# Other PSUM buffers, half steps, 128-wide stationary blocks and another order of work in an attention-plus-ELU-MLP kernel

## Chip, cores and metric

One core of one Trainium2 chip. The metric is the device time of one execution in microseconds (us). Profiled spans are some 2 us shorter than timed executions.

## The reference

Sliding-window attention with ALiBi over 8 batches of 8 heads, then a two-layer perceptron with ELU:

```python
scores = q @ k.T / sqrt(64)            # batch 8, heads 8, sequence 576, head dim 64
bias = slopes * -abs(rel)              # slopes 2**-(h+1)
mask = (rel >= 0) & (rel < 128)
attn = softmax(where(mask, scores + bias, -1e9))
x = (attn @ v)                         # to 4608 tokens x 512
h = x @ w_in                           # 512 -> 2048
g = where(h > 0, h, exp(min(h, 0)) - 1)
out = g @ w_out                        # 2048 -> 512, float32
```

The input is random; results are compared with this.

## The kernel before

Work goes out in slots. In each slot TensorE (PE) does a *hidden* step (16 matmuls of 128 columns or 8 of 256 into one 512-column PSUM bank), then attention tasks, then an *output* step. A hidden step is followed by an exponential on ScalarE (ACT), a clamp on GpSimd (POOL), and the ELU on VectorE (DVE), which reads the same PSUM bank once more. The ELU of step s-1 is issued after hidden step s.

```python
ps_s = tile_pool(name="ps_s", bufs=1, space=PSUM)     # sp: scores, 4 banks, one tile
ps_v = ...bufs=1   # av       ps_o = ...bufs=1   # op
ps_h = tile_pool(name="ps_h", bufs=2, space=PSUM)     # hp: a tile of one bank, twice
sp = ps_s.tile([128, 4, 512], F32, name="sp", tag="sp")
# ... cut ...
def hidden(t, c0, w, f0, nf):
    p = hps[t, c0, f0] = ps_h.tile([128, 512], F32, name="hp", tag="hp")
    # ... matmuls into p ...
    nc.scalar.activation(e[:, 0:n], p[:, 0:n], AF.Exp)
    nc.gpsimd.tensor_scalar(out=e[:, 0:n], in0=e[:, 0:n], scalar1=1.0, scalar2=0.0, op0=ALU.min, op1=ALU.max)

def elu(t, c0, w, f0, nf):
    V.scalar_tensor_tensor(out=gs[t][...], in0=sh(es.pop((t, c0, f0))), scalar=1.0,
                           in1=sh(hps.pop((t, c0, f0))), op0=ALU.subtract, op1=ALU.max)

def values(b, i, gp):                                 # block 4 of a batch has 64 rows
    m = 128 if i < 4 else 64
    parts = ([(unit(b, 3), 128, 3, 128), (unit(b, 3), 192, 4, 64)] if i == 4 else ...)
    # ... nc.tensor.matmul(a[0:m, g, h2, :], e[0:kk, 2*gp+g, h2, c:c+m], VP[...][0:kk, ...]) ...

for s in range(min(slots), max(slots) + 1):
    for f, a in early.get(s, []): f(*a)               # attention exponentials
    if s in HID: hidden(*HID[s])
    if s - 1 in HID: elu(*HID[s - 1])
    for f, a in tasks.get(s, []): f(*a)
    if s in OUT: output(*OUT[s])
```

The softmax here doesn't subtract the row's maximum and nothing guards it: scores larger than these inputs give would overflow.

## Time and profile before

| | before |
|---|---|
| median of 3 executions | 360.79 us (360.69 to 361.33) |
| profiled span | 358.8 us |
| PE busy | 332.8 us, 93% |
| to the first hidden step | 18.12 us |
| first hidden step to first output step (slots 0 to 17) | 34.08 |
| slots 18 to 33 | 18.34 |
| slots 34 to 47 (batch 1's block) | 34.30 |
| slot 48 to the start of the last hidden step (slot 159) | 237.78 |
| rest | 16.18 |

The stages are read from the order of time on PE: the start of the first hidden matmul, the first output matmul, and so on.

### The profile page before, as it was taken

How to read it: one execution, taken by the hardware profiler on the slowest of the kernel's cores; microseconds unless marked ns; L12 is line 12 of the kernel's file. 1: busy time of each engine (PE TensorE's matmuls, PEld its weight loads, DVE VectorE, ACT ScalarE, POOL GpSimd, SP SyncE). 2: the span in 40 equal slices, each digit the busy share in tenths (PEclk: the TensorE clock that was granted, in tenths of full speed). 3: DMA queues.
4: the chain of work that ended last, by engine and by line, in shares of the span. 5: the costliest groups of instructions: out<-in, count | busy, mean ns of one | idle time of the engine just before them, and what ended most of it. 6: DMA issues, size and time to landing. Idle time of an engine off the chain costs nothing.

```text
span 358.8 us, 8891 instructions
## 1 busy us (share of the span) xinstructions
PE 332.8 (93%) x3706; PEld 230.7 (64%) x3706; DVE 223.3 (62%) x443; ACT 175.4 (49%) x313; POOL 172.8 (48%) x261
## 2 busy tenths in 40 slices
PE   8898879856999999999999999999999999999994
PEld 8687664445676666766667666666677666666641
DVE  5445536479668866786669756786679566654320
ACT  1645344554455545554666255555556365533421
POOL 9336459254466536562666456562656133332320
PEclk9879999999999999999999999999999999999999
DMA  9998349995577838994899649991999311111011
GB/s 111 195 188 110 36 41 134 190 151 38 65 107 94 91 64 104 107 97 69 93 112 94 78 67 123 100 98 39 136 115 102 61 45 46 46 45 38 29 60 58
DMA packets 97320, 32.10 MB, mean 89 GB/s; under 512 B 87040, under 2 KB 92672, under 8 KB 97280
## 3 DMA queue, kind: packets, MB, share of 16 engines
q0 software_dynamic: 76480, 18.36, 60.2%
q1 hardware_dynamic: 20800, 13.18, 13.1%
q8 instruction: 29, 0.48, 0.5%
q14 instruction: 11, 0.09, 0.1%
HBM read 36.70 MB, written 9.44 MB: 129 GB/s over the span
## 4 chain that ended last, share of the span: by engine, by line
PE 68%; DVE 10%; ACT 8%; DMA 4%; issue 4%; POOL 4%; ACTq 0%; DVEq 0%; POOLq 0%
PE hp L225 26%; PE op L247 25%; PE av L189 9%; DVE g L238 5%; ACT EX L173 5%; PE sp L167 4%; POOL e L231 3%; ACT e L230 3%; DMA wo<-in_moe_w_out_dram 2%; DMA out_dram<-ob 2%; PE spare L257 2%; DVE EX L179 2%; DVE KT L127 1%; PE sp L148 1%; DVE QT L127 1%
## 5 line engine op out<-in xcount | busy, mean ns | idle before, releaser
L231 POOL TENSOR_SCALAR e<-e 128x512 f32<-128x512 f32 x144 | 93.5, 650 | 167.1 <-ACT e L230 166.3
L225 PE MATMUL hp<-xT,wi 128*128 128x256 f16 (+3 forms) x1600 | 151.0, 243 | 12.8 <-DVE g L238 9.4
L225 PEld LDWEIGHTS <-wi 128*128 128x128 f16 x1600 | 122.3, 98 | 52.4 <-issue 17.3
L247 PE MATMUL op<-wo,g 128*128 128x512 f16 x576 | 145.3, 379 | 2.6 <-ACT ob L251 1.4
L230 ACT ACTIVATE e<-hp 128x512 f32<-128x512 f32 x144 | 87.2, 605 | 115.0 <-PE hp L225 112.6
L238 DVE SCALAR_TENSOR_TENSOR g<-e,hp 128x512 f16<-128x512 f32 x144 | 96.9, 673 | 55.9 <-POOL e L231 54.4
L247 PEld LDWEIGHTS <-g 128*128 128x128 f16 x576 | 50.7, 97 | 48.2 <-issue 7.8
L173 ACT ACTIVATE EX<-sp 128x512 f16<-128x512 f32 (+1 forms) x121 | 69.8, 634 | 15.9 <-PE sp L167 10.1
L179 DVE TENSOR_TENSOR EX<-EX,TAB 128x1024 f16<-128x1024 f16 x56 | 39.1, 699 | 29.5 <-ACT EX L173 29.5
L189 PE MATMUL av<-VP,EX 128*128 128x65 f16 (+1 forms) x576 | 44.4, 200 | 2.5 <-ACT EX L173 1.3
L189 PEld LDWEIGHTS <-EX 128*128 128x128 f16 (+1 forms) x576 | 34.7, 100 | 12.6 <-issue 3.1
L251 ACT COPY ob<-op 128x512 f32<-128x512 f32 x36 | 21.1, 586 | 40.6 <-PE op L247 38.4
L198 DVE TENSOR_TENSOR xn<-av,rden 128x256 f16<-128x256 f32 (+1 forms) x80 | 33.8, 423 | 2.7
L93 POOL DMA_DIRECT2D VP<-in_v_dram x40 | 35.0, 879 | 0.7 <-issue 0.6
L197 DVE RECIPROCAL rden<-av 128x4 f32<-128x4 f32 (+1 forms) x80 | 14.1, 176 | 24.1 <-PE av L189 23.9
L127 DVE STREAM_TRANSPOSE KT<-st 128x576 f16<-128x576 f16 x28 | 22.5, 814 | 0.0
L127 DVE STREAM_TRANSPOSE QT<-st 128x576 f16<-128x576 f16 x28 | 22.3, 807 | 0.0
L167 PE MATMUL sp<-QT,KT 32*128 32x256 f16 (+2 forms) x560 | 18.3, 250 | 2.7 <-ACT EX L173 2.7
L87 POOL DMA_DIRECT2D st<-in_q_dram x28 | 19.1, 681 | 2.7 <-DMA wo<-in_moe_w_out_dram 2.1
L87 POOL DMA_DIRECT2D st<-in_k_dram x28 | 19.2, 689 | 0.7 <-DMA VP<-in_v_dram 0.6
L167 PEld LDWEIGHTS <-KT 32*128 32x128 f16 (+1 forms) x560 | 10.5, 95 | 5.9 <-issue 4.2
L257 PE MATMUL spare<-ident 128*128 128x128 f16 x90 | 6.6, 249 | 1.6 <-DVE ident L282 1.6
(33 smaller groups left out, 60.8 us busy)
## 6 DMA issues: line engine op xcount, KB each, us to landing
out_dram<-ob SPq DMA_DIRECT2D x36, 256.0 KB, 2.4
VP<-in_v_dram POOLq DMA_DIRECT2D x32, 128.0 KB, 4.0
st<-in_k_dram POOLq DMA_DIRECT2D x28, 144.0 KB, 3.6
st<-in_q_dram POOLq DMA_DIRECT2D x28, 144.0 KB, 3.5
wi<-in_moe_w_in_dram POOLq DMA_DIRECT2D x4, 512.0 KB, 11.1
wo<-in_moe_w_out_dram POOLq DMA_DIRECT2D x4, 512.0 KB, 6.1
VP<-in_v_dram POOLq DMA_DIRECT2D x8, 64.0 KB, 3.2
xT<-xn SPq DMA_TRANSPOSE x32, 3.4
```

Source lines behind the costliest of these rows:

```text
L87: nc.gpsimd.dma_start(st[b][32 * g:32 * g + 32, w, :, :, :, :].rearrange("p h n j d -> p (h n) (j d)"), (q, k)[w][b, 2 * g:2 * g + 2, :, : ...
L93: nc.gpsimd.dma_start(VP[b % 2][0:p, n, :, 0:D], v[b, :, 128 * n:128 * n + p, :].rearrange("h p d -> p h d"))
L127: V.transpose(o, st[b][:, w, h2, :, :, 32 * dh:32 * dh + 32])
L167: nc.tensor.matmul(sp[0:m, g, 256 * h2 + o:256 * h2 + o + n], kt[r, h2, dh, 128 * kb:128 * kb + m], qt[r, h2, dh, q0:q0 + n], start=dh == ...
L173: nc.scalar.activation(unit(b, u)[:, g0:g1, :, c0:c1], sp[:, g0:g1, :].rearrange("p g (h c) -> p g h c", h=2)[:, :, :, c0:c1], AF.Exp, sca ...
L179: V.tensor_tensor(out=e, in0=e, in1=TAB[:, int(u == 3), 2 * gp:2 * gp + 2, :, :], op=ALU.mult)
L189: nc.tensor.matmul(a[0:m, g, h2, :], e[0:kk, 2 * gp + g, h2, c:c + m], VP[b % 2][0:kk, n, 4 * gp + 2 * g + h2, 0:D + 1], start=j == 0, sto ...
L225: nc.tensor.matmul(p[:, l * w + u0:l * w + u1], w_in_sb[:, c, fc * 128:(fc + 1) * 128], xT[:, c, x0:x0 + u1 - u0], start=(c == 0), stop=(c ...
L230: nc.scalar.activation(e[:, 0:n], p[:, 0:n], AF.Exp)
L231: nc.gpsimd.tensor_scalar(out=e[:, 0:n], in0=e[:, 0:n], scalar1=1.0, scalar2=0.0, op0=ALU.min, op1=ALU.max)
L238: V.scalar_tensor_tensor(out=gs[t][:, f0:f0 + nf, c0:c0 + w], in0=sh(es.pop((t, c0, f0))), scalar=1.0, in1=sh(hps.pop((t, c0, f0))), op0=A ...
L247: nc.tensor.matmul(o, gs[t][:, fc, ts * 128:(ts + 1) * 128], w_out_sb[:, fc, :], start=(fc == 0), stop=(fc == NFC - 1))
```

## The change

The intent: hidden steps of batch 0 get four PSUM buffers instead of two (two banks of sp are lent to them, and scores of batch 0 then use the other two, four heads at a time); in batch 1's block each step is cut in two halves, each with half a bank; all stationary blocks are made 128 columns wide, with zeroed padding, so that matmuls of the last block need not change form; the second transposes of batch 0 move behind the first hidden step, and several loads are issued earlier.

```diff
-    ps_h = ctx.enter_context(tc.tile_pool(name="ps_h", bufs=2, space=PSUM))
+    ps_h = ctx.enter_context(tc.tile_pool(name="ps_h", bufs=1, space=PSUM))
...
     sp = ps_s.tile([128, 4, 512], F32, name="sp", tag="sp")
+    hp = ps_h.tile([128, 2, 512], F32, name="hp", tag="hp")
...
-            parts = ([(unit(b, 3), 128, 3, 128), (unit(b, 3), 192, 4, 64)] if i == 4 else
+            parts = [(3, 128, 3), (3, 192, 4)] if i == 4 else [(i, 0, i)] + ...
-                            a[0:m, g, h2, :], e[0:kk, 2 * gp + g, h2, c:c + m],
-                            VP[b % 2][0:kk, n, 4 * gp + 2 * g + h2, 0:D + 1],
+                        nc.tensor.matmul(a[:, x, h2, :], ex_[u][:, c:c + 128], VP[b % 2][:, n, 2 * g + h2, 0:D + 1],
...
-        def hidden(t, c0, w, f0, nf):
-            p = hps[t, c0, f0] = ps_h.tile([128, 512], F32, name="hp", tag="hp")
+        def hidden(t, c0, w, f0, nf, p):
+            hps[t, c0, f0] = p
-            e = es[t, c0, f0] = work.tile([128, 512], F32, name="e", tag="e")
+            e = es[t, c0, f0] = work.tile([128, 512], F32, name="e", tag="e", bufs=6)
...
+        BUF = [hp[:, 0, :], hp[:, 1, :], sp[:, 2, :], sp[:, 3, :]]
+        HALF = [hp[:, i, 256 * j:256 * j + 256] for i in range(2) for j in range(2)]
         for s, (sub, f) in enumerate(first):
-            HID[s] = (0, 128 * sub, 128, 4 * f, 4)
+            HID[s] = [(0, 128 * sub, 128, 4 * f, 4, BUF[s % 2 if s < 4 else s % 4])]
...
-            HID[34 + f] = (1, 64, 128, 4 * f, 4)
+            HID[34 + f] = [(1, 64, 128, 4 * f + 2 * i, 2, HALF[2 * (f % 2) + i]) for i in range(2)]
...
-                HID[16 * t + 16 + j] = (t, 256 * (j // 8), 256, 2 * (j % 8), 2)
+                HID[16 * t + 16 + j] = [(t, 256 * (j // 8), 256, 2 * (j % 8), 2, BUF[j % 2])]
```

Left out: scores and exponentials of batch 0 by half, the padding memsets, the new slots of tasks and loads, output buffers given as banks.

More of the change, by code (lines that the diff above doesn't have):

```diff
@@ L61 @@
     QT = [one([128, 2, 2, S], F16, f"QT{i}") for i in range(2)]
-    KT = [one([128, 2, 2, S], F16, f"KT{i}") for i in range(2)]
+    kt_ = [one([128, 4 * S + 64], F16, f"KT{i}") for i in range(2)]
+    KT = [t[:, 0:4 * S].rearrange("p (a b s) -> p a b s", a=2, b=2) for t in kt_]
     Q0, K0 = [t[0].rearrange("p a b s -> p (a b) s") for t in (QT, KT)]
     VP = [one([128, 5, H, VW], F16, f"VP{i}") for i in range(2)]
-    EX = [one([128, 4, 2, 256], F16, f"EX{i}") for i in range(4)]
+    ex_ = [one([128, 2048 + 64], F16, f"EX{i}") for i in range(4)]
+    EX = [t[:, 0:2048].rearrange("p (g h c) -> p g h c", g=4, h=2) for t in ex_]
     w_in_sb = one([128, 4, FF], F16, "wi")
@@ L103, in load_wo, with turn_first @@
             moe_w_out[512 * i:512 * i + 512, :].rearrange("(c p) d -> p c d", p=128))
-    def turn_first(w, part, half, tag):
-        pool = {"hp": ps_h, "av": ps_v, "op": ps_o}[tag]
+    def turn_first(w, part, half, bank):
         n, nh = ((64, 2), (32, 4))[part]
-        t = pool.tile([128, nh, 6, n], F16, name="tp", tag=tag)
+        if bank is None:
+            bank = ps_o.tile([128, DO], F32, name="tp", tag="op")
+        t = bank.bitcast(F16)[:, 0:nh * 6 * n].rearrange("p (x j r) -> p x j r", x=nh, j=6)
         r = slice(64 * part, 64 * part + n)
@@ L138, in unit @@
             return EX[u]
-        def scores(b, u):
-            qt, kt = QT[b % 2], KT[b % 2]
-            parts = ([(0, u, 128 * u, 256)] if u < 3 else [(0, 3, 384, 192), (192, 4, 512, 64)])
-            if b == 0:
-                for part, (o, kb, q0, n) in enumerate(parts):
-                    m = 128 if kb < 4 else 64
-                    for h2 in range(2):
-                        for g in range(4):
-                            nc.tensor.matmul(
-                                sp[0:m, g, 256 * h2 + o:256 * h2 + o + n], SI[:, 2 * g + h2, 0:m], RB[:, 0:n],
-                                start=part == h2 == 0, stop=False, skip_group_check=True)
-                for o, kb, q0, n in parts:
-                    m = 128 if kb < 4 else 64
-                    for x in range(4):
-                        for hh in range(2):
-                            r, h = slice(64 * hh, 64 * hh + 64), 4 * hh + x
-                            c = 256 * (h % 2) + o
-                            nc.tensor.matmul(
-                                sp[0:m, h // 2, c:c + n], K0[r, x, 128 * kb:128 * kb + m], Q0[r, x, q0:q0 + n],
-                                start=False, stop=True, skip_group_check=True)
-                return
-            for o, kb, q0, n in parts:
-                m = 128 if kb < 4 else 64
@@ new lines, in blocks, with first_scores @@
+        def blocks(u):
+            return [(0, u, 128 * u, 256)] if u < 3 else [(0, 3, 384, 192), (192, 4, 512, 64)]
+        def first_scores(u, half, d):
+            heads = [(x, hh) for x in (2 * half, 2 * half + 1) for hh in range(2)]
+            for part, (o, kb, q0, n) in enumerate(blocks(u)):
+                for x, hh in heads:
+                    c = 256 * (x % 2) + o
+                    nc.tensor.matmul(sp[:, 2 * d + hh, c:c + n], SI[:, 4 * hh + x, :], RB[:, 0:n],
+                                     start=part == x % 2 == 0, stop=False, skip_group_check=True)
+            for o, kb, q0, n in blocks(u):
+                for x, hh in heads:
+                    r, c = slice(64 * hh, 64 * hh + 64), 256 * (x % 2) + o
+                    k0 = x * S + 128 * kb
+                    nc.tensor.matmul(sp[:, 2 * d + hh, c:c + n], kt_[0][r, k0:k0 + 128], Q0[r, x, q0:q0 + n],
+                                     start=False, stop=True, skip_group_check=True)
@@ L163, in scores, with first_expo @@
+        def first_expo(u, half, d, c0, c1):
+            nc.scalar.activation(
+                unit(0, u)[:, half::2, :, c0:c1],
+                sp[:, 2 * d:2 * d + 2, :].rearrange("p g (h c) -> p g h c", h=2)[:, :, :, c0:c1], AF.Exp, scale=0.125)
+        def scores(b, u):
+            for o, kb, q0, n in blocks(u):
                 for h2 in range(2):
@@ L166, in scores, with expo @@
                             r = slice(32 * g, 32 * g + 32)
+                            k0 = (2 * h2 + dh) * S + 128 * kb
                             nc.tensor.matmul(
-                                sp[0:m, g, 256 * h2 + o:256 * h2 + o + n], kt[r, h2, dh, 128 * kb:128 * kb + m],
-                                qt[r, h2, dh, q0:q0 + n], start=dh == 0, stop=dh == 1,
+                                sp[:, g, 256 * h2 + o:256 * h2 + o + n], kt_[b % 2][r, k0:k0 + 128],
+                                QT[b % 2][r, h2, dh, q0:q0 + n], start=dh == 0, stop=dh == 1,
                                 tile_position=(32 * g, 0))
-        def expo(b, u, g0, g1, c0=0, c1=256):
-            nc.scalar.activation(
-                unit(b, u)[:, g0:g1, :, c0:c1],
-                sp[:, g0:g1, :].rearrange("p g (h c) -> p g h c", h=2)[:, :, :, c0:c1], AF.Exp, scale=0.125)
+        def expo(b, u, g):
+            nc.scalar.activation(unit(b, u)[:, g, :, :], sp[:, g, :].rearrange("p (h c) -> p h c", h=2),
+                                 AF.Exp, scale=0.125)
         def weigh(b, u, gp):
@@ L179, in weigh, with values @@
             V.tensor_tensor(out=e, in0=e, in1=TAB[:, int(u == 3), 2 * gp:2 * gp + 2, :, :], op=ALU.mult)
-        def values(b, i, gp):
+        def values(b, i, part):
             m = 128 if i < 4 else 64
-            parts = ([(unit(b, 3), 128, 3, 128), (unit(b, 3), 192, 4, 64)] if i == 4 else
-                     [(unit(b, i), 0, i, 128)] + ([(unit(b, i - 1), 128, i - 1, 128)] if i else []))
+            banks = (part, part + 2) if b == 0 else (2 * part, 2 * part + 1)
+            parts = [(3, 128, 3), (3, 192, 4)] if i == 4 else [(i, 0, i)] + ([(i - 1, 128, i - 1)] if i else [])
@@ L185, in values @@
             a = ps_v.tile([128, 2, 2, D + 1], F32, name="av", tag="av")
-            for g in range(2):
+            for x, g in enumerate(banks):
                 for h2 in range(2):
-                    for j, (e, c, n, kk) in enumerate(parts):
-                        nc.tensor.matmul(
-                            a[0:m, g, h2, :], e[0:kk, 2 * gp + g, h2, c:c + m],
-                            VP[b % 2][0:kk, n, 4 * gp + 2 * g + h2, 0:D + 1],
-                            start=j == 0, stop=j == len(parts) - 1)
@@ L193, in values @@
-            if gp == 0:
-                xnt[b, i] = work.tile([128, 2, 4, D], F16, name="xn", tag="xn", bufs=6)
-            r = work.tile([128, 4], F32, name="rden", tag="rden", bufs=2)
-            af = a.rearrange("p g h d -> p (g h) d")
-            V.reciprocal(out=r[0:m, :], in_=af[0:m, :, D])
-            V.tensor_tensor(out=xnt[b, i][0:m, gp, :, :], in0=af[0:m, :, 0:D],
-                            in1=r[0:m, :].unsqueeze(2).broadcast_to([m, 4, D]), op=ALU.mult)
+                    for j, (u, c, n) in enumerate(parts):
+                        c += 512 * g + 256 * h2
+                        nc.tensor.matmul(a[:, x, h2, :], ex_[u][:, c:c + 128], VP[b % 2][:, n, 2 * g + h2, 0:D + 1],
+                                         start=j == 0, stop=j == len(parts) - 1)
@@ new lines, in values @@
+            if part == 0:
+                xnt[b, i] = work.tile([128, 4, 2, D], F16, name="xn", tag="xn", bufs=6)
+            o = xnt[b, i][0:m, part::2, :, :] if b == 0 else xnt[b, i][0:m, 2 * part:2 * part + 2, :, :]
+            r = work.tile([128, 2, 2], F32, name="rden", tag="rden", bufs=2)
+            V.reciprocal(out=r[0:m], in_=a[0:m, :, :, D])
+            V.tensor_tensor(out=o, in0=a[0:m, :, :, 0:D], in1=r[0:m].unsqueeze(3).broadcast_to([m, 2, 2, D]),
+                            op=ALU.mult)
@@ L203, in turn @@
             o = (b * S + 128 * i) % RING
-            x = xnt.pop((b, i)).rearrange("p a h d -> p (a h d)")
+            x = xnt.pop((b, i)).rearrange("p g h d -> p (g h d)")
             if dma:
@@ L232, in hidden, with elu @@
                                     op0=ALU.min, op1=ALU.max)
-        def elu(t, c0, w, f0, nf):
+        def elu(t, c0, w, f0, nf, p):
             if t not in gs:
@@ L240, in elu, with output @@
                 in1=sh(hps.pop((t, c0, f0))), op0=ALU.subtract, op1=ALU.max)
-        def output(t, ts, f0, pool=None, tag="op"):
+        def output(t, ts, f0, bank=None, av=False):
             if f0 == 0:
-                ops[t, ts] = (pool or ps_o).tile([128, DO], F32, name="op", tag=tag)
+                ops[t, ts] = (bank if bank is not None else ps_v.tile([128, DO], F32, name="oa", tag="av") if av else
+                              ps_o.tile([128, DO], F32, name="op", tag="op"))
             o = ops[t, ts]
@@ L274 @@
         load_wi(1)
-        for n in (2, 3, 4):
-            load_v(0, n)
+        load_v(0, 2)
         load_wi(2)
+        load_v(0, 3)
+        load_v(0, 4)
         load_wi(3)
+        load_wo(0)
+        load_wo(1)
         rowf = one([128, 1], F32, "rowf")
@@ L284 @@
             V.memset(VP[i][:, :, :, D:D + 1], 1.0)
+            V.memset(VP[i][64:128, 4, :, 0:D], 0.0)
+            V.memset(kt_[i][:, 4 * S:4 * S + 64], 0.0)
+        for e in ex_:
+            V.memset(e[:, 2048:2112], 0.0)
         ra = one([128, 512], F32, "ra")
@@ L299 @@
         warm(90)
-        turn_first(1, 0, 0, "hp")
-        turn_first(0, 0, 0, "hp")
-        turn_first(1, 0, 1, "op")
-        turn_first(0, 0, 1, "av")
-        scores(0, 0)
-        expo(0, 0, 0, 2, 0, 128)
-        expo(0, 0, 2, 4, 0, 128)
-        expo(0, 0, 0, 4, 128, 256)
+        turn_first(1, 0, 0, hp[:, 0, :])
+        turn_first(0, 0, 0, hp[:, 1, :])
+        turn_first(1, 0, 1, None)
+        turn_first(0, 0, 1, sp[:, 3, :])
+        for half in range(2):
+            first_scores(0, half, half)
+        for half in range(2):
+            first_expo(0, half, half, 0, 128)
+        for half in range(2):
+            first_expo(0, half, half, 128, 256)
         values(0, 0, 0)
-        turn_first(1, 1, 0, "hp")
-        turn_first(0, 1, 0, "hp")
         values(0, 0, 1)
-        scores(0, 1)
-        expo(0, 1, 0, 4, 0, 128)
-        expo(0, 1, 0, 4, 128, 256)
         turn(0, 0, False)
-        values(0, 1, 0)
+        for half in range(2):
+            first_scores(1, half, half)
+        for half in range(2):
+            first_expo(1, half, half, 0, 128)
         early, tasks, HID, OUT = {}, {}, {}, {}
@@ L325, in before @@
             early.setdefault(s, []).append((f, a))
-        first = [(0, 0), (0, 1), (1, 0), (1, 1), (2, 0), (2, 1), (0, 2), (1, 2),
-                 (2, 2), (3, 0), (3, 1), (3, 2), (0, 3), (1, 3), (2, 3), (3, 3)]
+        BUF = [hp[:, 0, :], hp[:, 1, :], sp[:, 2, :], sp[:, 3, :]]
+        HALF = [hp[:, i, 256 * j:256 * j + 256] for i in range(2) for j in range(2)]
+        first = [(0, 0), (0, 1), (1, 0), (1, 1), (0, 2), (1, 2), (2, 0), (2, 1),
+                 (2, 2), (0, 3), (1, 3), (2, 3), (3, 0), (3, 1), (3, 2), (3, 3)]
         for s, (sub, f) in enumerate(first):
-            HID[s] = (0, 128 * sub, 128, 4 * f, 4)
+            HID[s] = [(0, 128 * sub, 128, 4 * f, 4, BUF[s % 2 if s < 4 else s % 4])]
         for f in range(2):
-            HID[16 + f] = (1, 0, 64, 8 * f, 8)
+            HID[16 + f] = [(1, 0, 64, 8 * f, 8, BUF[2 + f])]
         for f in range(4):
             for ts in range(4):
-                pool, tag = ((ps_o, "op"), (ps_v, "av"), (ps_h, "hp"), (ps_h, "hp"))[ts]
-                OUT[18 + 4 * f + (ts if f < 3 else (1, 0, 2, 3)[ts])] = (0, ts, 4 * f, pool, tag)
+                OUT[18 + 4 * f + (ts if f < 3 else (1, 0, 2, 3)[ts])] = (
+                    0, ts, 4 * f, BUF[ts - 2] if ts > 1 else None, ts == 1)
         for f in range(4):
-            HID[34 + f] = (1, 64, 128, 4 * f, 4)
-            HID[40 + f] = (1, 256, 128, 4 * f, 4)
-            HID[44 + f] = (1, 384, 128, 4 * f, 4)
+            HID[34 + f] = [(1, 64, 128, 4 * f + 2 * i, 2, HALF[2 * (f % 2) + i]) for i in range(2)]
+            HID[40 + f] = [(1, 256, 128, 4 * f + 2 * i, 2, HALF[2 * (f % 2) + i]) for i in range(2)]
+            HID[44 + f] = [(1, 384, 128, 4 * f, 4, BUF[f % 2])]
         for f in range(2):
-            HID[38 + f] = (1, 192, 64, 8 * f, 8)
+            HID[38 + f] = [(1, 192, 64, 8 * f + 4 * i, 4, HALF[2 * f + i]) for i in range(2)]
         for t in range(2, NTB):
             for j in range(16):
-                HID[16 * t + 16 + j] = (t, 256 * (j // 8), 256, 2 * (j % 8), 2)
+                HID[16 * t + 16 + j] = [(t, 256 * (j // 8), 256, 2 * (j % 8), 2, BUF[j % 2])]
         for t in range(1, NTB):
@@ L348 @@
                 OUT[16 * t + 26 + j] = (t, j // 4, 4 * (j % 4))
+        at(0, turn_first, 1, 1, 0, hp[:, 1, :])
+        at(0, values, 0, 1, 0)
+        at(0, turn_first, 0, 1, 0, None)
         at(0, values, 0, 1, 1)
-        at(0, scores, 0, 2)
-        before(1, expo, 0, 2, 0, 4, 0, 128)
+        for half in range(2):
+            before(1, first_expo, 1, half, half, 128, 256)
         at(1, turn, 0, 1, False)
-        before(2, expo, 0, 2, 0, 4, 128, 256)
-        at(2, values, 0, 2, 0)
-        at(3, values, 0, 2, 1)
@@ L358 @@
-        at(3, scores, 0, 3)
-        before(4, expo, 0, 3, 0, 4, 0, 128)
-        before(4, turn, 0, 2, False)
-        before(5, expo, 0, 3, 0, 4, 128, 256)
-        at(5, values, 0, 3, 0)
-        at(6, values, 0, 3, 1)
-        at(7, values, 0, 4, 0)
-        at(7, turn, 0, 3, False)
-        at(8, values, 0, 4, 1)
-        at(9, turn, 0, 4, False)
+        at(1, first_scores, 2, 0, 0)
+        at(1, first_scores, 2, 1, 1)
+        before(2, first_expo, 2, 0, 0, 0, 128)
+        before(2, first_expo, 2, 1, 1, 0, 128)
@@ new lines @@
+        before(3, first_expo, 2, 0, 0, 128, 256)
+        before(3, first_expo, 2, 1, 1, 128, 256)
+        at(3, values, 0, 2, 0)
+        at(3, values, 0, 2, 1)
+        at(3, first_scores, 3, 0, 0)
+        at(4, turn, 0, 2, False)
+        before(5, first_expo, 3, 0, 0, 0, 128)
+        before(6, first_expo, 3, 0, 0, 128, 256)
+        at(6, first_scores, 3, 1, 0)
+        at(7, values, 0, 3, 0)
+        before(7, first_expo, 3, 1, 0, 0, 128)
+        before(8, first_expo, 3, 1, 0, 128, 256)
@@ L368 @@
+        at(8, values, 0, 3, 1)
+        at(9, values, 0, 4, 0)
+        at(9, turn, 0, 3, False)
+        at(10, values, 0, 4, 1)
+        at(11, turn, 0, 4, False)
         for h in range(H):
             at(17 + h, table, h)
-        at(0, load_wo, 0)
-        at(2, load_wo, 1)
-        for n, s in enumerate((3, 4, 5, 6)):
+        for n, s in enumerate((2, 3, 5, 5)):
             at(s, load_qk, 1, 1, n)
-        for n, s in enumerate((8, 11, 14, 16)):
+        for n, s in enumerate((6, 8, 11, 14)):
@@ L377 @@
             at(s, load_qk, 1, 0, n)
-        at(17, load_wo, 2)
-        at(18, load_v, 1, 0)
-        at(19, load_v, 1, 1)
-        at(20, load_wo, 3)
-        for n in range(3):
-            at(21 + n, load_v, 1, 2 + n)
+        at(15, load_wo, 2)
+        at(16, load_wo, 3)
+        for n in range(5):
+            at(17 + n, load_v, 1, n)
         for n in range(4):
-            at(19 + n, turn_qk, 1, 1, *divmod(n, 2))
-            at(23 + n, turn_qk, 1, 0, *divmod(n, 2))
+            at(18 + n, turn_qk, 1, 1, *divmod(n, 2))
+            at(22 + n, turn_qk, 1, 0, *divmod(n, 2))
@@ L391 @@
             for g in range(4):
-                before(a + 1 + (2 * g) // 3, expo, 1, u, g, g + 1)
+                before(a + 1 + (2 * g) // 3, expo, 1, u, g)
             at(a + 2, weigh, 1, u, 0)
@@ L409 @@
                 for g in range(4):
-                    before(a + 1 + g // 2, expo, b, u, g, g + 1)
+                    before(a + 1 + g // 2, expo, b, u, g)
                 at(a + 1, weigh, b, u, 0)
@@ L432 @@
                 f(*a)
-            if s in HID:
-                hidden(*HID[s])
-            if s - 1 in HID:
-                elu(*HID[s - 1])
+            for step in HID.get(s, []):
+                hidden(*step)
+            for step in HID.get(s - 1, []):
+                elu(*step)
             for f, a in tasks.get(s, []):
```

## The prediction

> **What bounds the kernel now.** I read the page first, then busy time by stage, then the waits inside the stages, then the order of time on TensorE (PE). The kernel works in slots: one step of the first layer (hidden, L225), the ELU of the step before, attention tasks, one step of the second layer (output, L247).
>
> Page, parts 1 and 2:
>
> ```profile
> PE 332.8 (93%) x3706; PEld 230.7 (64%) x3706; DVE 223.3 (62%) x443; ACT 175.4 (49%) x313; POOL 172.8 (48%) x261
> PE   8898879856999999999999999999999999999994
> PEclk9879999999999999999999999999999999999999
> ```
>
> PE is the bound from the 11th slice on; only the first quarter has holes. No other engine is over 62%. Busy time by stage (columns: stretch, length, then busy us of PE, weight load, DVE, ACT, POOL, granted clock, DMA share, GB/s), cut at the first hidden step, the first output, batch 1's block (slot 34), slot 42, slot 48 and the last hidden step:
>
> ```profile
> 0.00:18.12 18.12, 15.23 (x334) 13.02 (x335) 8.76 (x24) 7.15 (x9) 11.33 (x22) 0.91 1.25 153
> 18.12:52.20 34.08, 27.95 (x444) 24.25 (x442) 17.08 (x37) 14.32 (x22) 16.60 (x27) 0.95 0.75 96
> 52.20:70.54 18.34, 16.32 (x114) 7.44 (x111) 9.95 (x18) 9.51 (x19) 11.96 (x17) 1.00 1.45 145
> 70.54:92.70 22.16, 14.94 (x304) 12.69 (x303) 18.11 (x36) 12.35 (x24) 10.06 (x15) 1.00 0.78 97
> 92.70:104.84 12.14, 12.03 (x137) 8.29 (x137) 7.58 (x17) 5.87 (x12) 5.88 (x10) 1.00 0.73 100
> 104.84:343.50 238.66, 236.36 (x2341) 160.77 (x2341) 160.69 (x313) 123.85 (x227) 116.37 (x171) 1.00 0.68 81
> ```
>
> From 92.7 to 343.5 PE is busy 99%: there the time is what PE issues, nothing else. In 70.5 to 92.7 DVE (18.1 of 22.2) is nearer the bound than PE. In 18 to 52 neither is full: waits rule. The timeline of PE in the long stage shows what its work costs:
>
> ```profile
> 122.76 0.41 PE L189 MATMUL av<-VP,EX 128*128 128x65 f16 x8
> 123.01 1.02 PE L247 MATMUL op<-wo,g 128*128 128x512 f16 x4
> 126.50 1.04 PE L225 MATMUL hp<-xT,wi 128*128 128x256 f16 x8
> 127.47 1.24 PE L189 MATMUL av<-VP,EX 128*64 128x65 f16 x8
> 128.64 1.04 PE L247 MATMUL op<-wo,g 128*128 128x512 f16 x4
> ```
>
> Start to start, eight ordinary value matmuls take 123.01 - 122.76 = 0.25 us, 31 ns each. The eight for the last, 64-row block of a batch start 0.10 late (127.47 after a hidden step that issues in 0.87) and take 1.17. A closer look shows why: the two forms alternate, with 0.14 to 0.15 us from one to the next:
>
> ```profile
> 127.62 0.36 PE L189 MATMUL av<-VP,EX 64*64 64x65 f16 x2
> 127.76 0.36 PE L189 MATMUL av<-VP,EX 128*64 128x65 f16 x2
> ```
>
> Narrowness alone is not it: in batch 0's scores eight 64-column blocks of one form run together and load in 0.33 us, 41 ns each:
>
> ```profile
> 27.53 0.33 PEld L148 LDWEIGHTS <-SI 128*64 128x64 f16 x8 [0.16 <-issue]
> ```
>
> The waits of 18 to 52 us and of 70.5 to 92.7 us (total, times, longest) show the hidden buffers coming back late, and in the second stretch one chain: an output transfer, held up, blocks an ACT copy, behind it an exponential, behind it PE:
>
> ```profile
> PE hp L225 <- DVE g L238: 4.8, 8, 1.0
> ...
> PE sp L167 <- ACT EX L173: 2.5, 1, 2.5
> ACT ob L251 <- DMA out_dram<-ob: 2.2, 1, 2.2
> ```
>
> In slots 10 to 17 the hidden steps start at 41.80, 43.16, 44.96, 46.32, 48.11 us: 1.58 a slot, for 0.9 of work. A step plus ACT 0.60, POOL 0.61 and DVE 0.69 with hand-overs is 3.1 us, over two buffers 1.58.
>
> **What the Trainium skill says.** (1) "TensorEngine Tiling (Array Packing)", Tiling Modes, Key Properties: changing the tiling mode, not just the tile, drains TensorE. The trace agrees: 146 ns where row or column size changes at every matmul, 31 where it doesn't. (2) "TensorE: Matmul & The Clock Gate", Weight-path perf modes: the fast weight load needs 128 columns, so padding could help by that as well; the 41 ns above say that this part is small here. (3) The same page, Part 1, The HAM clock gate: a PE with little to do for some 3.4 us falls to half clock. The trace agrees: granted clock 0.50 in 15 to 21 us. (4) "PSUM — Partial Sum Buffer", PSUM bank collisions raise a hardware error: two engines may not be in one bank and quadrant at once. This matters for the half steps, which put two halves in one bank; no run yet shows what it costs.
>
> **The change part by part.**
>
> *All blocks 128 wide.* Every value matmul becomes 128*128. A last-block call falls from 0.10 + 1.17 = 1.27 to 0.25, saved 1.02; where scores follow, from 1.26 to 0.34, saved 0.92. In the long stage there are 2 calls in each of 6 batches: 12 x 0.98 = 11.8. The scores of unit 3 take 0.69 against 0.55 for other units; I give back 0.07 in each of 6: 0.4. PE is on the path there, so it all counts. DVE: at 126.27 it had caught up, waiting for POOL, and idled 1.79 before the slow call's result, so it can follow; average load goes from 67% to 71%. For its local queues I take off 0.4. **Long stage: -11.8.** Batch 1's two calls (91.56, 94.59) count below, batch 0's two are PE time as well (-1.8, below). The filling memsets (about 1.3 us of DVE by my estimate) lie in DVE's 1.76 us wait for the iota.
>
> *Batch 0: four heads at a time, second transposes after the first step, four buffers.* The first hidden step starts at 18.12, behind two groups of 96 transposes, scores of units 0 and 1, and three exponentials. New path: transposes end at 9.9; scores half by half to 11.3; exponentials to 12.4; values, DVE 0.6, turn 0.6, copy 0.42: 14.2; meanwhile scores of unit 1 (2 us, at half clock 3) hold PE to 16.2. So 1.9 earlier. From there to slot 18 PE has: 18 hidden x 0.9 = 16.2; 8 value calls 3.1; moved transposes 1.9; scores of units 2 and 3 4.0; turns 1.6: 26.8. With four buffers in slots 4 to 17 the 3.1 us chain allows 0.78 a slot, under PE's 0.9; POOL, with 0.61 a slot and five DMA issues of 0.7 to 0.8 in ten slots, needs 0.98. I add 2.0 for the half clock, which the gap of PE between 11.3 and 13.5 will bring again, and 0.4 for waits: 29.2. Slot 18 at 16.2 + 29.2 = 45.4, against 52.2. **First part: -6.8.**
>
> *Issues in other slots.* The second-layer weights were waited for twice (0.41 and 0.67 before outputs): the second half goes out at slots 15 and 16, before V, and both waits go. Ahead of slot 34 I leave the ACT and PSUM hand-over around slot 31 (0.9 us), which the order keeps. **Output stretch: -1.2**, 0.1 for the shorter queue. The wait for the output transfer (2.2) should fall to 0.5 or so, as batch 2's loads, issued at 59 to 68 us in its way, go out well before relative to a less crowded queue.
>
> *Half steps in slots 34 to 43.* Two 256-column instructions for each of 512. My estimates from rows of the profile: DVE 0.42 each (a 256-column PSUM read takes 425 ns) against 0.673, so +0.17 a slot; ACT 0.40 each (610 ns at 512 and 1022 at 1024), +0.2; POOL 0.40, +0.2. Ten slots: +1.7 on DVE, the fullest engine here. If one bank is kept to one engine, the second half's matmuls wait for the first half's exponential: 0.45 + 0.2 + 0.40 + 0.45 = 1.5 us in PE in place of 0.9, and where an attention exponential stands ahead on ACT, more. So: stall -1.7, DVE +1.7, ordering +0.8, the two last-block calls -1.5 (one of them beside a DVE queue). **Batch 1 block: -0.7.**
>
> Sum: -6.8 - 1.2 - 0.7 - 11.8 = -20.5, and 360.8 - 20.5 = **340.3 us**.
>
> **The rivals.** *A: DVE takes over.* If DVE is what sets slots with transposes, some of the 11.8 comes back as waits of hidden for the ELU. For: slots 51 to 57 show DVE without a gap and waits of 0.2. Against: it has caught up one slot before the slow calls. It would make 343 to 346. *B: the half steps stall PE bank by bank*, and each slot takes 2.7 instead of 2.2: +4, 344 to 345. For: the bank rule and the full DVE; against: PE has slack there. *C: the start runs at full clock and the half steps pipeline freely*: 2 from the clock, 2 from the block, and the transfer stall gone: 334 to 336. *D: narrow blocks cost by width and the drain stays*, because scores in 32-row tiles still alternate with 128-row work: then the 11.8 hardly shows and 352 results. Against it stand the 41 ns.
>
> **Range and chances.** The long stage is measured on PE itself, +-1. The first part is a chain of my own sums, +-3; the block +-3. Together some +-5, with rivals A and B above and C below: 334 to 347. Faster by 2% means under 353.6: even with no gain before 104 us the last-block calls alone give 349, so 0.96; within 2% 0.03; slower 0.01.
>
> **What would show it.** Right: value matmuls all 128*128 and 0.25 us per eight; the stretch from slot 48 to the last hidden step 11 to 12.5 shorter than 238.7; hidden steps of slots 10 to 17 at 0.9 to 1.0 apart; first hidden near 16, first output near 45, no wait for the second-layer weights. Wrong: hidden waiting for the ELU more than 1.2 us in the long stage (A); PE idle between the halves of a step, slots 34 to 43 over 24 us (B); or last-block values still near 1.2 us (D).

## The result

| | before | after |
|---|---|---|
| median | 360.74 us (4 executions) | 442.14 us (440.69 to 445.3, 4 executions) |
| to the first hidden step | 18.12 | 21.91 |
| slots 0 to 17 | 34.08 | 45.16 |
| slots 18 to 33 | 18.34 | 18.81 |
| slots 34 to 47 | 34.30 | 47.67 |
| slot 48 to last hidden step | 237.78 | 290.22 |
| rest | 16.18 | 16.13 |

The ratio is 1.226 (95% interval 1.220 to 1.233). The change is slower by 81 us, where 20 us faster was forecast, and the prediction gave slower a chance of 0.01. Two thirds of the loss (52.4) lie in the long stage, the stage that the prediction held to be the safest.

The page after, parts 1 and 2:

```profile
PE 343.2 (78%) x3706; PEld 232.1 (53%) x3706; DVE 226.3 (51%) x461; ACT 179.1 (41%) x330; POOL 169.5 (39%) x271
PE   7785669766788888778888877778888877787775
PEclk9678999965599999999999999999999999999999
```

No engine got more work to speak of: DVE 226 us for 223, ACT 179 for 175, PE the same 3706 matmuls (343 us for 333; the difference arose where the granted clock was lower, see below). PE is down to 78% busy, evenly over the whole long stage, so it waits in every slot. The busy time of two stages (columns as in the prediction: stretch, length, busy us of PE, weight load, DVE, ACT, POOL, clock, DMA share, GB/s):

```profile
85.88:118.43 32.55, 22.49 (x305) 19.08 (x305) 17.29 (x40) 12.06 (x29) 11.79 (x23) 0.59 0.38 37
133.55:424.80 291.25, 235.93 (x2341) 154.58 (x2341) 162.49 (x312) 125.27 (x227) 110.23 (x170) 1.00 0.48 66
```

In the long stage PE does the same 236 us of work as before in 291. What it waits for is in the waits of the whole run (us in total, times, longest; PEld is the weight load, and "issue" means that it waited for nothing that the profile shows). First the changed kernel, then the kernel before:

```profile
DVE g L246 <- ACT e L238: 171.5, 137, 4.4
PEld L233 <- issue: 101.6, 115, 1.7
PE hp L233 <- DVE g L246: 64.7, 99, 1.5
```

```profile
DVE g L238 <- POOL e L231: 54.4, 76, 1.9
PE hp L225 <- DVE g L238: 9.4, 20, 1.0
```

Before, the ELU on DVE waited for POOL's clamp, which makes its input, and PE waited 9.4 us in all for the ELU. Now the ELU waits for an *exponential on ACT*. The timeline of one slot shows which one:

```profile
391.13 1.03 PE L233 MATMUL hp<-xT,wi 128*128 128x256 f16 x8 [0.37 <-DVE g L246]
392.20 0.60 ACT L238 ACTIVATE e<-hp 128x512 f32<-128x512 f32 x1 [0.78 <-PE hp L233]
392.88 0.61 POOL L239 TENSOR_SCALAR e<-e 128x512 f32<-128x512 f32 x1 [1.90 <-ACT e L238]
392.89 0.69 DVE L246 SCALAR_TENSOR_TENSOR g<-e,hp 128x512 f16<-128x512 f32 x1 [1.27 <-ACT e L238]
393.64 1.03 PE L233 MATMUL hp<-xT,wi 128*128 128x256 f16 x8 [0.37 <-DVE g L246]
```

The ELU at 392.89 starts together with POOL's clamp of the step just computed, so it can't be this step's ELU: it is that of the step before, whose clamped input had been ready for 1.9 us (POOL's idle time before its next clamp). It has nothing to take from the exponential at 392.20, which reads the *other* bank. Yet it starts 0.09 us after that exponential ends, and the next hidden step starts 0.06 after the ELU. PE, ACT and DVE take turns: 1.03 + 0.60 + 0.69 plus three hand-overs is 2.51 us a slot, the distance from 391.13 to 393.64. Before, slots without attention were 1.74 apart and slots with it 2.0 to 3.0:

```profile
330.46 1.04 PE L225 MATMUL hp<-xT,wi 128*128 128x256 f16 x8
331.33 1.03 PE L247 MATMUL op<-wo,g 128*128 128x512 f16 x4
332.19 1.04 PE L225 MATMUL hp<-xT,wi 128*128 128x256 f16 x8
```

Ahead of the long stage the granted clock took part as well: 0.59 in slots 34 to 41, in the first of the two stretches above, and 0.91 in slots 0 to 17. Up to slot 42 PE was busy 85.5 us against 74.4 before, with the same 1196 matmuls. In r2 below, with nothing changed but the tiles, the clock in slots 34 to 47 is 1.00. So part of the loss outside the long stage came by way of the clock; no run takes the two apart. In the long stage the clock was 1.00 before and after.

### The profile page after: what moved, and what is told of

It is laid out like the page before. It is cut to its first block, busy times and chain, and to the rows that moved or that the text cites. A ratio compares the mean times of both kernels' runs of the same rounds, so it can differ in the third digit from the quotient of the medians.

```text
span 439.9 us, 9104 instructions
## 1 busy us (share of the span) xinstructions
PE 343.2 (78%) x3706; PEld 232.1 (53%) x3706; DVE 226.3 (51%) x461; ACT 179.1 (41%) x330; POOL 169.5 (39%) x271
## 4 chain that ended last, share of the span: by engine, by line
PE 50%; ACT 22%; DVE 19%; issue 6%; DMA 1%; DVEq 1%; ACTq 0%; POOL 0%; POOLq 0%
PE hp L233 29%; DVE g L246 17%; ACT e L238 16%; PE op L256 8%; ACT EX L181 4%; PE sp L175 3%; PE av L198 2%; PE spare L266 2%; PE sp L233 2%; PE sp L154 1%; DMA out_dram<-ob 1%; PE hp L256 1%; ACT ob L260 1%; PE sp L160 1%; PE oa L256 1%
## 5 line engine op out<-in xcount | busy, mean ns | idle before, releaser
L233 PEld LDWEIGHTS <-wi 128*128 128x128 f16 x1600 | 127.9, 102 | 133.8 <-issue 101.6
L239 POOL TENSOR_SCALAR e<-e 128x512 f32<-128x512 f32 (+1 forms) x154 | 90.0, 584 | 250.4 <-ACT e L238 242.1
L246 DVE SCALAR_TENSOR_TENSOR g<-e,hp 128x512 f16<-128x512 f32 (+1 forms) x146 | 93.9, 650 | 161.3 <-ACT e L238 161.3
L238 ACT ACTIVATE e<-hp 128x512 f32<-128x512 f32 (+1 forms) x146 | 83.2, 570 | 180.6 <-PE hp L233 176.7
L256 PE MATMUL op<-wo,g 128*128 128x512 f16 x528 | 134.7, 380 | 1.4 <-ACT ob L260 1.4
L181 ACT ACTIVATE EX<-sp 128x512 f16<-128x512 f32 x112 | 61.7, 609 | 8.3 <-issue 4.5
L198 PE MATMUL av<-VP,EX 128*128 128x65 f16 x576 | 32.5, 199 | 6.1 <-DVE xn L205 4.7
L198 PEld LDWEIGHTS <-EX 128*128 128x128 f16 x576 | 28.4, 101 | 9.1 <-DVE xn L205 4.7
L260 ACT COPY ob<-op 128x512 f32<-128x512 f32 x33 | 19.3, 586 | 33.9 <-PE op L256 33.9
L164 ACT ACTIVATE EX<-sp 128x512 f16<-128x512 f32 x16 | 8.8, 598 | 10.8 <-PE sp L160 10.0
L233 PE MATMUL sp<-xT,wi 128*128 128x128 f16 (+1 forms) x160 | 8.5, 208 | 5.6 <-DVE g L246 3.0
```

The lines of the kernel that those rows point to most:

```text
L181: nc.scalar.activation(unit(b, u)[:, g, :, :], sp[:, g, :].rearrange("p (h c) -> p h c", h=2), AF.Exp, scale=0.125)
L198: nc.tensor.matmul(a[:, x, h2, :], ex_[u][:, c:c + 128], VP[b % 2][:, n, 2 * g + h2, 0:D + 1], start=j == 0, stop=j == len(parts) - 1)
L233: nc.tensor.matmul(p[:, l * w + u0:l * w + u1], w_in_sb[:, c, fc * 128:(fc + 1) * 128], xT[:, c, x0:x0 + u1 - u0], start=(c == 0), stop=(c ...
L246: V.scalar_tensor_tensor(out=gs[t][:, f0:f0 + nf, c0:c0 + w], in0=sh(es.pop((t, c0, f0))), scalar=1.0, in1=sh(hps.pop((t, c0, f0))), op0=A ...
L256: nc.tensor.matmul(o, gs[t][:, fc, ts * 128:(ts + 1) * 128], w_out_sb[:, fc, :], start=(fc == 0), stop=(fc == NFC - 1))
```

## The experiments

**Theory T1.** Both hp banks now belong to one tile, and in the program as built, accesses of different engines to one PSUM tile are put in order by semaphores, whatever bank they touch. **Rival T2.** The loss comes from another part: the new order of issue, the padding, the half steps, or the six e buffers.

The lists of instructions, each with the semaphores that it waits for, already differ. Before, and in r2 below, the ELU waits for POOL alone; in the changed kernel for ACT too:

```
changed kernel:  ELU g<-e,hp [waits Activation, Pool]
r2, two tiles:   ELU g<-e,hp [waits Pool]
```

The traces name the semaphores too and agree: after 135 us, 112 of 113 ELUs of the changed kernel and 113 of 114 of r1 wait for ACT and POOL, all 99 of the kernel before and all 101 of r2 for POOL alone. A list tells no time, so each side was run.

### r1: the kernel before with hp as one tile of two banks

```diff
-    p = hps[t, c0, f0] = ps_h.tile([128, 512], F32, name="hp", tag="hp")
+    hp2 = ps_h.tile([128, 2, 512], F32, name="hp", tag="hp")   # once, pool bufs=1
+    p = hps[t, c0, f0] = next_hp()                             # hp2[:, 0, :], hp2[:, 1, :] in turn
```

(The early transposes and the outputs that borrow an hp buffer take it in the same turn.)

> The kernel before with one edit: its two hidden PSUM buffers become the two banks of one tile, used in turn. Theory T1 (accesses of different engines to one PSUM tile are put in order even where they touch different banks, so the ELU of step s-1 waits for the exponential of step s): hidden steps of the long stage 2.5 us apart where only 1.74 to 2.3 before, long stage near 290 instead of 238.7, whole kernel 410 to 435. Rival T2 (the loss comes from the other parts, new order, padding or half steps): within 1% of 361.

Measured: correct, 453.47 us, ratio 1.257 (1.253 to 1.260). This edit alone, with nothing else of the change, costs 93 us. Hidden steps at the end of the long stage, order of time on PE:

```profile
420.41 1.03 PE L235 MATMUL hp<-xT,wi 128*128 128x256 f16 x8 [0.61 <-DVE g L248]
421.28 1.03 PE L257 MATMUL op<-wo,g 128*128 128x512 f16 x4
422.91 1.03 PE L235 MATMUL hp<-xT,wi 128*128 128x256 f16 x8 [0.61 <-DVE g L248]
```

The distance is 2.50 us, as T1 says; the long stage takes 297.9. The total is above the expected range since slots 0 to 17 suffered more than I allowed (55.1 us in place of 34.1, with a granted clock of 0.67 there in place of 0.95). T2 is out as the main cause.

### r2: the changed kernel with hp as two tiles of one bank

```diff
-    hp = ps_h.tile([128, 2, 512], F32, name="hp", tag="hp")
+    hp = [ps_h.tile([128, 512], F32, name=f"hp{i}", tag=f"hp{i}") for i in range(2)]
```

(and `hp[:, i, :]` becomes `hp[i]`).

> The changed kernel with hp as two tiles of one bank each, sp left as one tile of four banks. T1: the long stage falls from 290 to about 227 (238.7 less 12 for the last-block values), whole kernel 360 to 378, since half steps and the two banks borrowed from sp still wait. T2: stays within 2% of 442.

Measured: correct, 353.68 us, ratio 0.980 (0.978 to 0.983) to before.

```profile
319.79 1.04 PE L233 MATMUL hp<-xT,wi 128*128 128x256 f16 x8
320.68 1.02 PE L256 MATMUL op<-wo,g 128*128 128x512 f16 x4
321.54 1.04 PE L233 MATMUL hp<-xT,wi 128*128 128x256 f16 x8
```

Hidden steps are 1.75 us apart without a wait, and the long stage takes 225.1: one allocation was worth 65 us there and 88 us in all. It came out better than expected because the stages before it fell too: slots 34 to 47 from 47.7 to 33.6, and the first output came at 59.1 us in place of 67.1. The same two banks, used by the same engines for the same work, gave right results without the order between them; so the results didn't need it.

### r4: every lent bank its own tile

```diff
-    sp = ps_s.tile([128, 4, 512], F32, name="sp", tag="sp")
+    spa = ps_s.tile([128, 2, 512], F32, name="spa", tag="spa")
+    sp = [spa[:, 0, :], spa[:, 1, :]] + [ps_s.tile([128, 512], F32, name=f"sp{i}", tag=f"sp{i}") for i in (2, 3)]
```

(on top of r2; the exponential of batch 0 over banks 2 and 3 is cut in two).

> The changed kernel with every borrowed bank its own tile: hp as two, sp as one of two banks and two of one (the exponential of batch 0 over the latter in two instructions). T1: as r2 and 5 to 10 us less, since slots 6 to 17 lose the waits between banks: 352 to 368; hidden steps of slots 10 to 17 about 1 us apart. T2: near 440. If slots 34 to 43 stay over 24 us, the half steps in one bank cost by themselves.

Measured: correct, 343.04 us, ratio 0.951 (0.947 to 0.956), better than the range given. The first output comes at 46.62 us, against 59.06 in r2 and 52.20 before: lending banks of the sp tile had the same fault, at 12 us, in part again by the clock (0.89 in slots 0 to 17 of r2, 1.00 in r4). From slot 10 to 14 the hidden steps are 1.07 us apart, as expected. Slots 34 to 47 take 35.0, over 34.3 before, and slots 34 to 43 take 26.8, over the 24 that was to tell of a cost of the half steps.

### r3: the kernel before with only the 128-wide blocks

```diff
-                     [(unit(b, 3), 128, 3, 128), (unit(b, 3), 192, 4, 64)] if i == 4
+                     [(3, 128, 3), (3, 192, 4)] if i == 4
-   nc.tensor.matmul(a[0:m, g, h2, :], e[0:kk, 2 * gp + g, h2, c:c + m], VP[b % 2][0:kk, n, ...])
+   nc.tensor.matmul(a[:, g, h2, :], ex_[u][:, c:c + 128], VP[b % 2][:, n, ...])
```

(with the padding and memsets of the change, and K blocks of 128 columns in the scores).

> The kernel before with only the 128-wide blocks. Drain theory of the prediction: last-block value calls fall from 1.27 to 0.25 us, 12 in the long stage, 2 in each of batches 0 and 1: 345 to 349. Rival (drain stays or DVE takes over): 353 to 361.

Measured: correct, 344.38 us, ratio 0.954 (0.951 to 0.956), 0.6 us better than the range given. The long stage is 225.4 in place of 237.8: 12.4 us for 12 last-block calls and 6 last score units, where 11.8 was predicted. One part alone does nearly as well as r4 with all of them; their times overlap (342.25 to 345.28 in r4, 343.98 to 345.43 here).

### r8: r3 with the last block narrow again, but of one form

```diff
-   a[:, g, h2, :], ex_[u][:, c:c + 128]
+   a[0:m, g, h2, :], ex_[u][:, c:c + m]
```

> r3 (the kernel before with 128-wide blocks) with the last block's value matmuls 64 columns wide again, but all of one form (128 rows by 64 columns). Drain theory: only the change into and out of that form costs, eight matmuls in about 0.33 to 0.40 plus 0.2 us, so 0.3 to 0.4 a call more than r3: 347 to 351. Rival (width itself, a slower weight load): 1.0 a call more, 357 to 361.

Measured: correct, 347.89 us, ratio 0.963 (0.958 to 0.968). The last-block call in r8:

```profile
124.26 0.44 PE L191 MATMUL av<-VP,EX 128*64 128x65 f16 x8
124.63 1.04 PE L249 MATMUL op<-wo,g 128*128 128x512 f16 x4
```

and the same call in r3:

```profile
124.48 0.41 PE L191 MATMUL av<-VP,EX 128*128 128x65 f16 x8
124.72 1.02 PE L249 MATMUL op<-wo,g 128*128 128x512 f16 x4
```

Eight narrow matmuls of one form take 0.37 us and come 0.09 late; eight wide ones 0.24 to 0.25, not late. So of the 1.02 us that a call lost before, about 0.81 is the alternation of forms, which "TensorEngine Tiling (Array Packing)", Key Properties, calls a drain, and 0.21 is what one run of the narrow form costs. The single starts in the trace split that: inside the run the narrow matmuls are 35 ns apart on average, the wide ones of r3 31; the step from the last narrow one to the output matmul takes 126 ns, and the way in is the 0.09. So nearly all of the 0.21 is two more changes of form, and width itself about 4 ns a matmul, 0.03 us a call. By "TensorE: Matmul & The Clock Gate", Weight-path perf modes, the fast weight load needs 128 columns; if these 4 ns are that, it is worth little here.

### r5, r6: whole steps in slots 34 to 43; more output tiles

```diff
# r5, on top of r4
-   HID[34 + f] = [(1, 64, 128, 4 * f + 2 * i, 2, HALF[2 * (f % 2) + i]) for i in range(2)]
+   HID[34 + f] = [(1, 64, 128, 4 * f, 4, BUF[f % 2])]        # slots 38 to 43 alike
# r6, on top of r5
-   ob = work.tile([128, DO], F32, name="ob", tag="ob")       # pool: 3
+   ob = work.tile([128, DO], F32, name="ob", tag="ob", bufs=5)
```

> r4 (every borrowed bank its own tile) with whole steps of 512 columns in slots 34 to 43 in place of the half steps. If the half steps cost by themselves (the second half's matmuls wait 0.47 us for the first half's exponential in the same bank, and two instructions stand for one on ACT, POOL, DVE): slots 34 to 47 fall from 35.0 us to 31 to 33, whole 339 to 341.5 against 343.0. If they help once the tiles are apart: 344 to 348.

> r5 with five output tiles in SBUF in place of three, so that the copy of the fourth output near slot 34 doesn't wait for the first one's transfer. If that transfer is on the path: the wait of the copy for the transfer goes and 0.5 to 2 us with it against r5, so 338 to 340.5. If the path goes elsewhere: within 0.5 of r5.

Measured: r5 339.87 us, ratio 0.939 (0.935 to 0.944); r6 338.76, ratio 0.937 (0.933 to 0.940); both correct. All of this lies in the ranges given. In r5 slots 34 to 47 take 32.2 although two waits of the kernel before came back there, the fourth output copy behind the first output's transfer and PE behind ACT:

```profile
PE sp L181 <- ACT EX L187: 2.2, 1, 2.2
ACT ob L266 <- DMA out_dram<-ob: 2.2, 1, 2.2
```

In r6 both are gone and these slots take 29.7. The times of r5 and r6 overlap, so the whole gain of the extra output tiles is not resolved by the times; in the profiles it is 2.5 us in these slots and 2.2 in the span, of which up to 1 us may be chance: r12, the same kernel as r6, takes 30.7 in these slots.

### r7, r9: half steps over two banks

```diff
-   HALF = [hp[i][:, 256 * j:256 * j + 256] for i in range(2) for j in range(2)]
+   HALF = [hp[i][:, 256 * j:256 * j + 256] for j in range(2) for i in range(2)]
# r9 also: five output tiles, and the ELU of slot 43 issued before hidden step 44
```

> r4 with the two halves of a half step in different banks (halves of one slot in banks 0 and 1, the next slot's in the other halves of the same banks). If the 0.47 us between halves is the order within one bank: these waits go and PE waits elsewhere for the ELU in the same bank; slots 34 to 43 shorter by 1 to 4 us, whole 339 to 342. If the loss of the half steps is DVE's and ACT's instruction count: unchanged, 342.5 to 344.

r7 gave a wrong result (relative error 0.065): hidden step 44 is a whole step, and wrote over a half of slot 43 before its ELU had read it. That was my mistake, not a finding; its time, 340.64 us, is not used.

> r7 (half steps over two banks) with the mistake of r7 mended (slot 44's whole step overwrote a half of slot 43 before its ELU had read it; the ELU of slot 43 now goes out first) and five output tiles: correct. If the order within one bank was most of what half steps cost: slots 34 to 47 at 29.5 to 31.5 us, within 0.6% of r12. If two instructions for one cost on DVE and ACT as well: 31.5 to 34, 1 to 3 us over r12.

> r4 (half steps in one bank) with five output tiles, beside r12 with whole steps on the same chip: if half steps in one bank cost 4 to 5 us in slots 34 to 47 once the output transfer's wait is out of both, 1.1 to 1.5% slower than r12; if their loss in r4 was chance of the chip, within 0.5%.

> r6 again (tiles apart, whole steps, five output tiles), to stand beside r9 and r11 on one chip: 336.5 to 339.5, ratio to before 0.933 to 0.940.

r11 is r4 with five output tiles (half steps in one bank), r12 is r6 once more, and r9, r11 and r12 ran on one chip. All are correct:

| | median us | ratio to before | slots 34 to 47, us |
|---|---|---|---|
| r12, whole steps | 338.82 | 0.937 (0.934 to 0.940) | 30.65 |
| r9, halves over two banks | 340.28 | 0.941 (0.938 to 0.944) | 31.70 |
| r11, halves in one bank | 342.36 | 0.947 (0.943 to 0.950) | 33.69 |

In r11 the largest wait of PE in these slots is between the halves, ten times. First r11, then r12:

```profile
PE hp L239 <- ACT e L244: 6.8, 10, 1.2
```

```profile
PE hp L239 <- DVE g L252: 2.5, 4, 0.9
```

So half steps in one bank cost some 3 us, less than the 4 to 5 expected, and r11's interval lies clear of r12's (r11 is 1.0% slower, just under the 1.1 to 1.5% expected). Putting the halves in different banks takes back about two thirds by the stage, each a single profile; the intervals of r9 and r11 overlap slightly. The remaining 1 us of r9 against r12 is not clear of the spread of the times or of this stage (29.7 in r6, 30.65 in r12, one kernel): r9's total fits both of its expectations, its stage the second alone, so whether two instructions for one cost anything by themselves stays open.

### r10: one tile, the ELU issued before the next step

```diff
+            for step in HID.get(s - 1, []): elu(*step)
             for step in HID.get(s, []): hidden(*step)
-            for step in HID.get(s - 1, []): elu(*step)
```

> The changed kernel, hp one tile, with the ELU of step s-1 issued before hidden step s instead of after it. T1 in full (PE, ACT and DVE take turns in the tile whatever the bank): a step can't begin before the ELU of the step before, so the whole chain of matmul 1.03, ACT 0.60, POOL 0.61, DVE 0.69 and hand-overs, 3.1 us, becomes the distance of hidden steps; long stage near 350, whole 490 to 515. If only readers of the tile take turns and a matmul into the other bank doesn't wait: ACT, POOL and DVE in turn, about 2.0 a step, long stage 230 to 245, whole 380 to 400.

This asks how far the order in one tile goes: only between its readers, or for PE as well.

```profile
508.02 1.03 PE L233 MATMUL hp<-xT,wi 128*128 128x256 f16 x8 [1.24 <-DVE g L246]
508.89 1.03 PE L256 MATMUL op<-wo,g 128*128 128x512 f16 x4
511.15 1.03 PE L233 MATMUL hp<-xT,wi 128*128 128x256 f16 x8 [1.24 <-DVE g L246]
```

Measured: correct, 536.68 us, ratio 1.486. Hidden steps are 3.13 us apart: the full chain, one step after the other. A matmul into bank 1 waits for the ELU that still reads bank 0. So all three engines take turns in the tile, as T1 has it; the alternative (2.0 us a step) is out. The total is above the range given: the long stage took 354.7, as expected, but slot 48 began only at 162.7, with a granted clock of 0.66 in slots 0 to 17 and 0.74 in slots 34 to 47.

## Why the prediction was wrong

**The step that failed** is "PE is on the path there, so it all counts", said of the long stage, together with "With four buffers in slots 4 to 17 the 3.1 us chain allows 0.78 a slot". Both rest on buffers that can be used independently, as the two of before could. The prediction took one tile of two banks for two buffers; in the diff this is the line where bufs=2 becomes bufs=1. With one tile, PE, ACT and DVE take turns, and the distance of hidden steps is the sum of the three instead of the largest: 2.51 us where slots without attention had taken 1.74. The ELU is issued after the next hidden step, so the wait is for the *next* step's exponential, one slot late. None of the four rivals had this. The sign that the prediction set for rival A, hidden waiting for the ELU for more than 1.2 us in the long stage, did come (1.3 at the longest, 55.9 in all against 1.2 before), but with another cause: rival A looked at DVE as too busy; DVE became late without more work. r1 shows the cause alone (+93 us), r2 its removal (-88 us).

**The parts, once freed of it** (r4 against before; stage lengths from the profiles):

| part | predicted | r4 |
|---|---|---|
| start to first output (slots to 17) | -6.8 | -5.6 |
| slots 18 to 33 | -1.2 | -1.4 |
| slots 34 to 47 | -0.7 | +0.7 |
| long stage | -11.8 | -12.4 |
| span in all | -20.5 | -18.3 |

- *Long stage*: the size was right, and r8 shows the mechanism, form changes and not width for the most part. Rivals A and D are refuted by r3.
- *Start*: the first hidden step came at 16.16 us where 16.2 was worked out. In later kernels with the same start it came at 16.5 to 17.0 and the first output at 48.2 to 49.0, with a granted clock of 0.95 in slots 0 to 17 of r12 against 1.00 in r4. So part of this gain varies from run to run, and 5.6 is its better end. That r4 comes within 1.2 us of the sum is luck in part. The stage from the first hidden step to the first output in r4 (columns as above):

```profile
16.16:46.62 30.46, 25.59 (x546) 23.36 (x545) 17.26 (x37) 16.80 (x33) 16.27 (x27) 1.00 1.02 124
```

The prediction had 26.8 of work, 2.0 for the half clock and 0.4 for waits, 29.2 in all. Here there is no half clock, as rival C had it, and PE is idle for 4.9 us, 1.2 of them in one wait for the ELU before slot 16. In r12 one stretch of half clock came (20.1 to 23.6 us), and the stage took 31.7. The prediction also read the half clock of the kernel before as that of a PE with little to do; in the 3.4 us before the clock fell at 14.9, the trace has PE busy for 82%, so that reading isn't shown.
- *Output stretch*: both waits for the second-layer weights went, as predicted. The wait for the output transfer fell to 0.6 us in r4, near the 0.5 forecast, but is 2.2 again in r5 with the same loads: the moved loads are not what shortened it.
- *Half steps*: rival B was right in kind. The matmuls of the second half wait for the first half's exponential in the same bank (0.47 us in most slots of r4, up to 1.8, 6.8 in all), and this costs about 3 us when the output transfer is out of the way (r11 against r12). The prediction had 0.8 for this ordering and 1.7 for DVE. DVE's busy time in slots 34 to 47 grew by only 0.9 (26.5 in r11, 25.6 in r12), and separating the banks took back about 2 of the 3 us, so the ordering was the larger term. "PSUM — Partial Sum Buffer" asks that two engines not be in one bank and quadrant at once, so that an order within a bank is needed for correctness by that page; no run here tried without it.

What stays open: why the program is built with an order by tile, where an order by bank would do, was not looked into. That the order is in the program is shown by its lists of waits and by r1, r2 and r10.

The version to keep is r6: every lent bank its own tile, whole steps, five output tiles. It takes 0.937 of the time of before in two rounds of runs on two chips.

## What to carry to other kernels

When a change joins buffers into one allocation, or lends part of an allocation to another use, look at the waits of every reader before counting the buffers as independent: two banks in one tile were worth less than two tiles by 88 us here. If a consumer of a PSUM buffer waits for an engine that doesn't make any of its inputs, the wait may be about storage; here splitting the allocation was the cure. Matmuls that alternate between array forms paid about 0.1 us at each change here, and padding them to one form cost no PE time: a wide matmul took 31 ns, a narrow one in a run of its own form 35.

## What the Trainium skill lacked or had wrong

- "PSUM — Partial Sum Buffer" advises to guard by bank and quadrant, by bank as the simple version. It doesn't warn that a program may end up guarded by tile, over several banks: 2.51 us a step where two tiles gave 1.73 to 1.75, 442 us in place of 354.
- The same page doesn't say what splitting one bank between two steps in flight costs: 0.47 us or more of PE wait between the halves, about 3 us in ten slots.
- "TensorEngine Tiling (Array Packing)" says that a change of tiling mode drains TensorE but gives no size: matmuls that change form each time were 146 ns apart, the same work in one narrow form 35, in full width 31; about 0.1 us a change.
- "TensorE: Matmul & The Clock Gate" ties the lower clock to idle stretches of some 3.4 us, with micro-idling as a second way and no size for it: in slots 34 to 41 of the changed kernel, where no named wait of PE was over 1.3 us, the granted clock fell to 0.50 at 91.8 us, after 3.4 us with PE 41% busy, and stayed there for 27.3 us, while PE 67% busy in the long stage of r10, in gaps of 1.24 us, kept 1.00.
